# The first batch's Newton steps on PE and ACT alone, and two pieces of G inside its first expert pass

## The chip, the cores and the metric

One core of a Trainium2 chip. The time is device microseconds of one execution of the whole program; the one before is the median of three runs. TensorE is called PE, VectorE DVE, ScalarE ACT, GpSimd POOL; SP issues most loads.

## The reference

Nystrom attention on 8 batches, 8 heads, 576 tokens of 64, feeding a mixture of 8 experts in which a token keeps its predecessor's expert where its local gate says so. All is in float32.

```python
q_lm, k_lm = means of 18 tokens each            # 32 landmarks
A, Bm, C = sm(q, k_lm), sm(q_lm, k_lm), sm(q_lm, k)
Z = Bm.T / (norm1(Bm) * norminf(Bm) + 1e-6)
for _ in range(6):
    Z = 2 * Z - Z @ Bm @ Z
x = A @ Z @ C @ v                                # 512 features a token
e = argmax(x @ w_gate) if fresh(x @ w_local) else the previous token's e
out = p[e] * (relu(x @ w1[e]) @ w2[e])
```

## The kernel before

Every batch goes through an attention (a list of some 33 small steps, `attention(b)`, L740) and an expert (`expert`, L525). Attention of batch 0 is written first; then a loop over batches writes the expert of batch b in 16 iterations, and between them, by due times (`at_time`, `run`), the attention steps of the next batches, some 24 iterations ahead. Each engine executes its instructions in one order of its own. That order isn't the order of the program text: a planner simulates the program and gives each engine the next instruction that is ready in its simulation, with earlier text preferred. So batch 1's attention runs in the gaps of batch 0's, and a long instruction may stand ahead of a short one that is ready a moment later.

Four heads lie side by side on 128 partitions, twice (g = 0, 1). In `scores_c` (L190) C's and Bm's scores are made, with maxima on DVE and exponentials on ACT: two of 288 columns (ec, L213), then one of 32 (bm, L215). `norms` (L248, L250 to L272) is a chain of some 13 short DVE operations from bm to nrc. `newton_first` (L279) makes E = I - c Bt Bt' (L283, L285, L286), and `newton_step` (L288) is run six times. It keeps [E | Z] side by side, multiplies both by E on PE (L292, eight 32x32 blocks, 16 matmuls in the trace), copies the new E with ACT (L295) and adds the product to Z with DVE (L296). Then `newton_w`, `newton_wt`, `newton_gate` (L298 to L321) make the matrix W that follows A; `gates`, `fresh`, `sticky`, `chosen`, `own` (L368 to L452) choose each token's expert and the batch's main one, whose number goes into `regs` (L439).

A itself: `scores_a` (L323), `a_max` (L338: a maximum on DVE, L341, and a subtraction on POOL, L342), `a_exp`, `a_norm`, `a_back`, and `a_split` (L362), which splits A into a high and a low part, ACT L364 and DVE L365.

With the number in `regs`, SP loads the expert's w1 in two halves of 1 MB (L463) and w2 in eight pieces (L498), each of which ACT and POOL split (L500, L501). `w_w1` (L466) multiplies W into w1: G, in four pieces q. Each piece is 32 matmuls (L477) into one bank of `pg` and one of `ph`; then ACT (L490) and DVE (L491) split each bank. The expert has two passes over tokens: 320 of them (blocks 2, 3 and half a block, 4), then 256. For each of 8 f, `mm1` (L504, six matmuls at L513) makes h = relu(G' A) in a `ph` bank, which takes piece f // 2 of G; one f later, L543 (blocks 0 to 3, banks `py`) and L548, L549 (block 4, bank `pg`, held over all f) multiply h by w2.

PSUM has 8 banks: `psa` 3 (name "one"), `ph` 2, `py` 2, `pg` 1. Batch 0's attention takes all of them in turn through `one`, since no expert runs yet; later ones have the three of `psa`. For batch 0 all four pieces of G stand in the text ahead of its expert (L814 to L820).

Of the kernel before, what the change touches and what calls it, by code (L numbers as in the profile page):

```python
# [9 lines left out]
F32 = mybir.dt.float32  # L10
# [12 lines left out]
M = 32  # L23
# [34 lines left out]
def nystrom_attn_then_sticky_moe(ctx, tc, qT, kT, v, wg, w12, out):  # L58
# [80 lines left out]
    spare = [(py, "py"), (ph, "ph"), (pg, "pg"), (py, "py"), (ph, "ph")]  # L139
    one = Banks(*[(psa, "one")] * 3, *spare)  # L140
# [7 lines left out]


# [40 lines left out]
    def scores_c(st, g):  # L190
# [57 lines left out]
    def norms(st):  # L248
# [23 lines left out]
        nc.vector.tensor_scalar_mul(nrc, rc, -1.0)  # L272
# [6 lines left out]
    def newton_first(st):  # L279


        ps = one.tile([P, 2, M])
# [5 lines left out]
    def newton_step(st, k):  # L288
# [4 lines left out]
        new = st["et"] = sm.tile([P, 2, 64], F32, name="et", bufs=4)  # L293
# [4 lines left out]
    def newton_w(st):  # L298
        pw = one.tile([P, 2, D])
# [5 lines left out]
    def newton_wt(b, st):  # L305

        pwt = one.tile([P, 2, P])
# [6 lines left out]
    def newton_gate(b, st):  # L314
        pg = one.tile([P, 2, 9])
# [7 lines left out]
    def scores_a(st, hf):  # L323
# [14 lines left out]
    def a_max(st):  # L338
# [23 lines left out]
    def a_split(st):  # L362
# [65 lines left out]
    def own(b, st):  # L428
# [10 lines left out]
        nc.vector.tensor_scalar(out=regs[:, b:b + 1], in0=mx[0:1], scalar1=-1.0, scalar2=float(E), op0=ALU.mult, op1=ALU.add)  # L439
# [26 lines left out]
    def w_w1(st, q):  # L466
# [3 lines left out]
        ps = [pool.tile([P, 512], F32, name=name)[:, 0:256] for pool, name in ((pg, "pg"), (ph, "ph"))]  # L470
# [33 lines left out]
    def mm1(st, f, s0, n):  # L504
# [13 lines left out]
        nc.scalar.activation(out=h[:, 0:n], in_=hp, func=AF.Relu)  # L518
        for a, e, to in ((0, m, 384), (m, n, 320)):
            if a < e:  # L520
                nc.vector.scalar_tensor_tensor(out=h[:, to:to + e - a], in0=hp[:, a:e], scalar=0.0,  # L521
                                               in1=h[:, a:e].bitcast(F32), op0=ALU.max, op1=ALU.subtract)
        return h
# [356 lines left out]
```

## Time and profile before

| | us |
|---|---|
| median of three runs | 549.0 (548.88 to 549.81) |
| the profiled execution | 545.98 |
| its span | 544.3 |
| PE busy in the span | 489.0 (90%) |
| DVE, ACT, POOL busy | 317.2, 214.5, 194.2 |
| batch 0's expert number in its register | 54.1 |
| first matmul of the expert passes | 76.4 |

The profile is one execution. Its rows give the start and the length of an instruction, or of a run of like ones, on its engine; what stands in square brackets is how long the engine stood idle ahead of it, and what ended that. The granted clock is a share of TensorE's full 2.4 GHz; 0.5 is its lower level, 1.2 GHz.

### The profile page before, as it was taken

Reading aid. Unit: us, or ns where it says so; the run is one execution under the profiler, and the core shown is the slowest. Engines: PE = TensorE matmul, PEld = TensorE weight load, DVE = VectorE, ACT = ScalarE, POOL = GpSimd, SP = SyncE. Lnnn points to the kernel's source line nnn. Section 1 sums busy time; section 2 is a strip of 40 time slices with the busy share of each in tenths; the row PEclk is TensorE's granted clock in tenths of the full one; section 3 lists DMA queues with packets and bytes.
Section 4 is the critical chain, followed back from the end, with each engine's and each line's share of the span. In section 5 each row is a group of like instructions: output and inputs, shape, how many; then the busy total and the mean of one; then the engine's idle time right before and its main releaser. Section 6 shows DMA issues by size and latency. Waiting matters only on the chain. (4 is left out here: it accounts for less than half of the span.)

```text
span 544.3 us, 12748 instructions
## 1 busy us (share of the span) xinstructions
PE 489.0 (90%) x4983; PEld 349.7 (64%) x4983; DVE 317.2 (58%) x997; ACT 214.5 (39%) x556; POOL 194.2 (36%) x203
## 2 busy tenths in 40 slices
PE   7456479999999999999999999999978996999995
PEld 2223147866676767767676677667766884678674
DVE  7878746845775478546873587346734558732321
ACT  2433342445334543356144623364234512441451
POOL 5562740643145322624162403132141402271240
PEclk9667569999999999999999999999998999899999
DMA  8745840981187214851195114711091108171220
GB/s 301 309 132 186 305 146 1 354 268 53 40 297 287 81 51 183 307 174 50 63 393 184 37 40 173 259 59 49 5 330 56 62 1 291 50 250 59 88 79 18
DMA packets 38607, 82.62 MB, mean 152 GB/s; under 512 B 3163, under 2 KB 4443, under 8 KB 37776
## 3 DMA queue, kind: packets, MB, share of 16 engines
q1 hardware_dynamic: 30656, 66.22, 35.0%
q10 hardware_dynamic: 6400, 10.49, 5.4%
q0 software_dynamic: 1488, 5.07, 2.4%
q8 instruction: 40, 0.66, 0.5%
q14 instruction: 23, 0.19, 0.1%
HBM read 66.34 MB, written 15.47 MB: 150 GB/s over the span
## 5 line engine op out<-in xcount | busy, mean ns | idle before, releaser
L543 PE MATMUL py<-wh,h 128*128 128x512 f32 x528 | 177.3, 408 | 3.3 <-ACT h L518 3.2
L501 POOL TENSOR_TENSOR wl<-raw,wh 128x512 fp32r<-128x512 f32 x72 | 97.5, 1358 | 189.4 <-ACT wh L500 189.2
L518 ACT ACTIVATE h<-ph 128x256 fp32r<-128x256 f32 (+2 forms) x136 | 55.1, 405 | 159.4 <-PE ph L513 141.5
L521 DVE SCALAR_TENSOR_TENSOR h<-ph,h 128x256 fp32r<-128x256 f32 (+1 forms) x200 | 64.3, 347 | 80.0 <-ACT h L518 79.2
L543 PEld LDWEIGHTS py<-wh,h 128*128 128x128 f32 x528 | 90.4, 188 | 24.6 <-ACT h L518 5.6
L543 PE MATMUL py<-wl,h 128*128 128x512 f32 x264 | 87.0, 395 | 0.0
L513 PE MATMUL ph<-ath,gh 128*128 128x320 f32 (+1 forms) x256 | 81.8, 320 | 0.7 <-DVE gl L491 0.7
L513 PE MATMUL ph<-atl,gh 128*128 128x320 f32 (+1 forms) x256 | 77.8, 304 | 0.0
L513 PE MATMUL ph<-ath,gl 128*128 128x320 f32 (+1 forms) x256 | 76.7, 300 | 0.0
L500 ACT CAST wh<-raw 128x512 fp32r<-128x512 f32 x72 | 44.7, 622 | 44.7 <-PE py L543 32.5
L513 PEld LDWEIGHTS ph<-ath,gh 128*128 128x128 f32 x256 | 49.2, 192 | 17.8 <-issue 8.4
L543 PEld LDWEIGHTS py<-wl,h 128*128 128x128 f32 x264 | 49.3, 188 | 11.7 <-issue 2.1
L342 POOL TENSOR_TENSOR sa<-sa,mxa 128x1152 f32<-128x1152 f32 x8 | 17.1, 2133 | 104.4 <-DVE mxa L341 86.4
L513 PEld LDWEIGHTS ph<-atl,gh 128*128 128x128 f32 x256 | 49.4, 193 | 5.7 <-issue 2.3
L513 PEld LDWEIGHTS ph<-ath,gl 128*128 128x128 f32 x256 | 49.3, 193 | 0.3
L477 PE MATMUL ph<-raw,wt 64*32 64x256 f32 x256 | 24.7, 425 | 12.8 <-DVE gl L491 5.4
L491 DVE TENSOR_TENSOR gl<-ph,gh 128x256 fp32r<-128x256 f32 x36 | 15.2, 422 | 29.6 <-ACT gh L490 29.6
L292 PEld LDWEIGHTS one<-et 32*32 32x32 f32 x704 | 13.8, 114 | 25.5 <-issue 10.5
L292 PE MATMUL one<-et 32*32 32x64 f32 (+1 forms) x704 | 22.7, 234 | 7.9 <-DVE et L296 7.9
L174 POOL TENSOR_TENSOR t<-q_t 128x288 f32<-128x288 f32 x28 | 21.4, 789 | 15.6 <-DMA q_t<-qT 10.9
L202 PE MATMUL one<-k_t,ql 64*32 64x288 f32 (+1 forms) x240 | 25.1, 482 | 1.6 <-ACT k_t L181 0.8
L548 PE MATMUL pg<-wh,h 128*128 128x512 f32 x64 | 26.4, 412 | 0.0
(286 smaller groups left out, 736.5 us busy)
## 6 DMA issues: line engine op xcount, KB each, us to landing
raw<-w SPq DMA_DIRECT2D x18, 1024.0 KB, 6.7
raw<-w SPq DMA_DIRECT2D x72, 256.0 KB, 6.2
v_t<-v SPq DMA_DIRECT2D x8, 1024.0 KB, 6.4
out<-ys ACTq DMA_DIRECT2D x32, 256.0 KB, 2.7
q_t<-qT SPq DMA_DIRECT2D x6, 1152.0 KB, 5.1
k_t<-kT SPq DMA_DIRECT2D x6, 1152.0 KB, 7.7
ad<-sa POOLq DMA_DIRECT2D x8, 576.0 KB, 7.4
q_t<-qT SPq DMA_DIRECT2D x4, 576.0 KB, 8.4
```

The lines of the kernel that those rows point to most:

```text
L174: nc.gpsimd.tensor_add(t9[:, i], src[:, a + i, :, 0:9], src[:, a + i, :, 9:18])
L202: nc.tensor.matmul(pc[hf][32 * c:32 * c + 32, 0:n], st["ql"][r, h // 2, :], st["k"][r, h // 2, 288 * hf:288 * hf + n], start=True, stop=True)
L292: each_place(lambda g, r: nc.tensor.matmul(pn[r, g, n0:64], et[r, g, 0:32], et[r, g, n0:64], start=True, stop=True))
L342: nc.gpsimd.tensor_tensor(out=sa, in0=sa, in1=mx.unsqueeze(2).broadcast_to([P, 2 * NJ, M]), op=ALU.subtract)
L477: mm = nc.tensor.matmul(ps[g][32 * c:32 * c + 32, :], st["wt"][r, g, 32 * c:32 * c + 32], w1[r, 2 * (q % 2):2 * (q % 2) + 2, a * P:a * P + ...
L500: nc.scalar.copy(out=wh, in_=raw)
L501: nc.gpsimd.tensor_tensor(out=wl, in0=raw, in1=wh.bitcast(F32), op=ALU.subtract)
L513: nc.tensor.matmul(hp, w[:, g, c], x[:, g, s0:s0 + n], start=(i == 0), stop=(i == 5))
L518: nc.scalar.activation(out=h[:, 0:n], in_=hp, func=AF.Relu)
L521: nc.vector.scalar_tensor_tensor(out=h[:, to:to + e - a], in0=hp[:, a:e], scalar=0.0, in1=h[:, a:e].bitcast(F32), op0=ALU.max, op1=ALU.sub ...
L543: nc.tensor.matmul(yps[k], h[:, part + i * P:part + i * P + P], w, start=(f == 0 and part == 0 and w is wh), stop=(f == NC2 - 1 and part = ...
L548: nc.tensor.matmul(yps[4], x, wh, start=(f == 0), stop=False)
```

## The change

Four things are altered. (1) Batch 0's Newton chain has banks of its own, the two of `ph`; everything else of batch 0's attention has the other six in turn. In its steps PE adds Z itself, by a second matmul with the identity into the same place, and one ACT copy takes the whole [E | Z]; there is no DVE instruction in the loop. (2) In `scores_c` of all batches bm's exponential comes first. `a_max` is ordered behind the last operation of the same batch's norms, and `a_split` behind the batch's expert number; both are orders on one engine or between engines without a wait where none is needed. (3) The pieces q = 2 and 3 of batch 0's G are written inside its first pass, at iterations 1 and 3. (4) For that, in batch 0's first pass `pg` isn't held over all f: the 64 tokens of block 4 get tiles of their own for each f (`hx`, eight buffers, with an ACT relu of their own), and all sixteen matmuls of block 4 come behind the last f.

```diff
-    spare = [(py, "py"), (ph, "ph"), (pg, "pg"), (py, "py"), (ph, "ph")]
-    one = Banks(*[(psa, "one")] * 3, *spare)
+    spare = [(py, "py"), (pg, "pg"), (py, "py")]
+    one = Banks(*[(psa, "one")] * 3, (py, "py"), (pg, "pg"), (py, "py"))
+    first_chain = Banks((ph, "ph"))
+
+    def chain(b):
+
+        return one if b else first_chain
...
+    marks = {}
+
+    def not_ahead_of(inst, mark):
+
+        if mark in marks:
+            tc.add_manual_dep(inst.ins, marks[mark], mybir.DependencyInfo(
+                mybir.DependencyClass.NoSync, mybir.DependencyReason.DATA), reason="order")
...
         nc.vector.tensor_scalar_mul(nm, mx[:, 2:4], -scale)
+        nc.scalar.activation(out=st["bm"][:, g, :], in_=pc[1][:, 288:320], func=AF.Exp, bias=nm[:, 1:2],
+                             scale=scale, accum_out=st["sb"][:, g:g + 1])
         ec = at.tile([P, 2, 288], F32, name=f"ec{g}")
...
-        nc.scalar.activation(out=st["bm"][:, g, :], in_=pc[1][:, 288:320], func=AF.Exp, bias=nm[:, 1:2],
-                             scale=scale, accum_out=st["sb"][:, g:g + 1])
...
-        nc.vector.tensor_scalar_mul(nrc, rc, -1.0)
+        marks["norms", b] = nc.vector.tensor_scalar_mul(nrc, rc, -1.0).ins.name
...
-        pn = one.tile([P, 2, 64])
+        pn = chain(b).tile([P, 2, 64])
+        new = st["et"] = sm.tile([P, 2, 64], F32, name="et", bufs=4)
+        if b == 0:
+            each_place(lambda g, r: (
+                nc.tensor.matmul(pn[r, g, n0:64], et[r, g, 0:32], et[r, g, n0:64], start=True, stop=False),
+                nc.tensor.matmul(pn[r, g, 32:64], id32[r], et[r, g, 32:64], start=False, stop=True)))
+            nc.scalar.copy(out=new[:, :, n0:64], in_=pn[:, :, n0:64])
+            return
...
-        nc.vector.reduce_max(out=mx, in_=sa, axis=AX.X)
+        not_ahead_of(nc.vector.reduce_max(out=mx, in_=sa, axis=AX.X), ("norms", b))
...
-        nc.scalar.copy(out=ah, in_=st["full"])
+        not_ahead_of(nc.scalar.copy(out=ah, in_=st["full"]), f"expert of batch {b}")
...
+        marks[f"expert of batch {b}"] = nc.vector.tensor_scalar(
+            out=regs[:, b:b + 1], in0=mx[0:1], scalar1=-1.0, scalar2=float(E), op0=ALU.mult, op1=ALU.add).ins.name
...
         h = fk.tile([P, 640], F32R, name="h", bufs=3)
-        nc.scalar.activation(out=h[:, 0:n], in_=hp, func=AF.Relu)
...
+        x = fk.tile([P, P], F32R, name="hx", bufs=NC2) if apart and m < n else h[:, 2 * P:3 * P]
+        e = m if apart else n
+        nc.scalar.activation(out=h[:, 0:e], in_=hp[:, 0:e], func=AF.Relu)
+        if e < n:
+            nc.scalar.activation(out=x[:, 0:64], in_=hp[:, m:n], func=AF.Relu)
...
                     if 4 in blocks:
 
-                        x = h[:, 2 * P:3 * P]
-                        nc.tensor.matmul(yps[4], x, wh, start=(f == 0), stop=False)
-                        nc.tensor.matmul(yps[4], x, wl, start=False, stop=(f == NC2 - 1))
+
+                        for ff in range(0 if f == NC2 - 1 else NC2, NC2) if apart else (f,):
+                            if 4 not in yps:
+                                yps[4] = pg.tile([P, DM], F32, name="pg")
+                            for w in w2[ff]:
+                                nc.tensor.matmul(yps[4], hs[ff][1], w, start=(ff == 0 and w is w2[ff][0]),
+                                                 stop=(ff == NC2 - 1 and w is w2[ff][1]))
...
         sts[0]["w1", hf] = load_w1(sts[0]["e"], hf)
-        for q in range(2 * hf, 2 * hf + 2):
-            w_w1(sts[0], q)
+        if hf == 0:
+            for q in range(2):
+                w_w1(sts[0], q)
...
-        gen = expert(st, w2s[b], PASSES, lambda k, yp, b=b, st=st: store(b, st, k, yp))
+        gen = expert(st, w2s[b], PASSES, lambda k, yp, b=b, st=st: store(b, st, k, yp), b == 0)
...
             run(b * CH + i)
+            if b == 0 and i in (1, 3):
+
+                w_w1(st, 2 + i // 2)
```

## Rows read from the trace of the kernel before

**Rows 1.** Busy time by stretches: us, engines' busy (instructions), clock, DMA share, GB/s.
```profile
38.60:54.20 15.60, 10.22 (x198) 5.82 (x202) 13.61 (x64) 6.93 (x23) 4.38 (x5) 0.79 0.44 161
54.20:76.42 22.22, 10.94 (x214) 4.70 (x206) 13.96 (x28) 9.78 (x28) 13.90 (x14) 0.58 0.78 270
65.40:71.45 6.05, 3.08 (x48) 1.29 (x48) 5.11 (x9) 1.42 (x4) 2.83 (x4) 0.50 1.03 368
116.20:172.76 56.56, 56.44 (x574) 40.51 (x567) 35.53 (x114) 24.30 (x65) 21.49 (x19) 1.00 0.48 168
```

**Rows 2.** Order of time, batch 0, softmax to norms: start, length, engine, line, tiles.
```profile
14.15 0.51 ACT L213 ACTIVATE ec<-py,nm 128x288 f32<-128x288 f32 x1
...
15.10 0.31 ACT L215 ACTIVATE bm<-ph,nm 128x32 f32<-128x32 f32 x1
...
15.66 1.34 DVE L341 TENSOR_REDUCE mxa<-sa 128x36 f32<-128x1152 f32 x1
...
17.07 2.13 POOL L342 TENSOR_TENSOR sa<-sa,mxa 128x1152 f32<-128x1152 f32 x1 [0.66 <-DVE rsc L244]
...
17.78 1.50 DVE L254 TENSOR_TENSOR bm<-bm,rsb 128x64 f32<-128x64 f32 x1
...
24.19 0.22 DVE L286 TENSOR_TENSOR et<-et,id 128x64 f32<-128x64 f32 x1
```

**Rows 3.** Two lines of the kernel in all batches: length in ns, least/median/most.
```profile
L254 DVE TENSOR_TENSOR bm<-bm,rsb x8: 216/224/1500, 17.8 to 375.2; 128x64 f32<-128x64 f32 x8
...
L365 DVE TENSOR_TENSOR atl<-at,ath x8: 1357/1359/3525, 30.4 to 428.1; 128x1152 fp32r<-128x1152 f32 x8
```

**Rows 4.** Order of time, batch 0's six Newton steps.
```profile
24.55 0.65 PE L292 MATMUL py<-et 32*32 32x64 f32 x16 [2.12 <-DVE et L286]
...
25.25 0.21 ACT L295 COPY et<-py 128x64 f32<-128x64 f32 x1 [0.78 <-PE py L292]
...
25.77 0.65 PE L292 MATMUL pg<-et 32*32 32x64 f32 x16
...
28.08 0.65 PE L292 MATMUL ph<-et 32*32 32x64 f32 x16
...
30.41 1.59 DVE L365 TENSOR_TENSOR atl<-at,ath 128x1152 fp32r<-128x1152 f32 x1 [0.25 <-ACT ath L364]
...
31.92 0.21 DVE L296 TENSOR_TENSOR et<-et,ph 128x64 f32<-128x64 f32 x1
...
36.84 0.43 PE L292 MATMUL ph<-et 32*32 32x32 f32 x16
...
38.34 0.21 DVE L296 TENSOR_TENSOR et<-et,ph 128x64 f32<-128x64 f32 x1
```

**Rows 5.** Order of time, from batch 0's expert number to its expert's first matmuls.
```profile
54.00 0.14 DVE L439 TENSOR_SCALAR regs<-mxc 1x1 int32<-1x1 f32 x1
...
60.06 0.63 PE L477 MATMUL ph<-raw,wt 64*32 64x256 f32 x1 [2.92 <-DMA raw<-w]
...
68.33 0.62 ACT L500 CAST wh<-raw 128x512 fp32r<-128x512 f32 x1 [3.43 <-DMA raw<-w]
...
69.72 0.42 DVE L491 TENSOR_TENSOR gl<-pg,gh 128x256 fp32r<-128x256 f32 x1
...
75.38 0.63 PE L477 MATMUL ph<-raw,wt 64*32 64x256 f32 x1 [2.83 <-DVE gl L491]
...
76.42 0.63 PE L513 MATMUL ph<-ath,gh 128*128 128x320 f32 x1
...
77.92 0.47 PE L513 MATMUL ph<-ath,gl 128*128 128x320 f32 x1
```

**Rows 6.** Order of time: batch 3's loads; batch 1's number, and its G.
```profile
45.36 0.34 SPq L154 DMA_DIRECT2D q_t<-qT  x1
...
100.17 0.14 DVE L439 TENSOR_SCALAR regs<-mxc 1x1 int32<-1x1 f32 x1
...
115.63 0.40 PE L477 MATMUL ph<-raw,wt 64*32 64x256 f32 x1
```

More of the change, by code (lines that the diff above doesn't have):

```diff
@@ L246, in c_v, with norms @@
         nc.vector.tensor_tensor(out=st["u"], in0=pv, in1=rs.unsqueeze(2).broadcast_to([P, 2, D]), op=ALU.mult)
-    def norms(st):
+    def norms(b, st):
         rs = sm.tile([P, 2], F32, name="rsb")
@@ L277, in each_place, with newton_first @@
                 fn(g, slice(32 * c, 32 * c + 32))
-    def newton_first(st):
-        ps = one.tile([P, 2, M])
+    def newton_first(b, st):
+        ps = chain(b).tile([P, 2, M])
         each_place(lambda g, r: nc.tensor.matmul(ps[r, g, :], st["bt"][r, g, :], st["bt"][r, g, :], start=True, stop=True))
@@ L296, in newton_step, with newton_w @@
         nc.vector.tensor_add(new[:, :, 32:64], et[:, :, 32:64], pn[:, :, 32:64])
-    def newton_w(st):
-        pw = one.tile([P, 2, D])
+    def newton_w(b, st):
+        pw = chain(b).tile([P, 2, D])
         each_place(lambda g, r: nc.tensor.matmul(pw[r, g, :], st["et"][r, g, 32:64], st["u"][r, g, :], start=True, stop=True))
@@ L305, in newton_wt @@
     def newton_wt(b, st):
-        pwt = one.tile([P, 2, P])
+        pwt = chain(b).tile([P, 2, P])
         for g in range(2):
@@ L314, in newton_gate @@
     def newton_gate(b, st):
-        pg = one.tile([P, 2, 9])
+        pg = chain(b).tile([P, 2, 9])
         for g in range(2):
@@ L502, in load_w2, with mm1 @@
         return wh, wl
-    def mm1(st, f, s0, n):
+    def mm1(st, f, s0, n, apart):
         hp = ph.tile([P, 512], F32, name="ph")[:, 0:n]
@@ L517, in mm1, with expert @@
         h = fk.tile([P, 640], F32R, name="h", bufs=3)
-        nc.scalar.activation(out=h[:, 0:n], in_=hp, func=AF.Relu)
[L519 to L523, printed above, removed]
-    def expert(st, w2, passes, store):
+        x = fk.tile([P, P], F32R, name="hx", bufs=NC2) if apart and m < n else h[:, 2 * P:3 * P]
[3 more added lines that the diff above has]
+            nc.scalar.activation(out=x[:, 0:64], in_=hp[:, m:n], func=AF.Relu)
+        nc.vector.scalar_tensor_tensor(out=h[:, 384:384 + m], in0=hp[:, 0:m], scalar=0.0, in1=h[:, 0:m].bitcast(F32),
+                                       op0=ALU.max, op1=ALU.subtract)
+        if m < n:
+            nc.vector.scalar_tensor_tensor(out=x[:, 64:128], in0=hp[:, m:n], scalar=0.0, in1=x[:, 0:64].bitcast(F32),
+                                           op0=ALU.max, op1=ALU.subtract)
+        return h, x
+    def expert(st, w2, passes, store, apart=False):
         before = None
@@ L530, in expert, with after @@
             for f in range(NC2):
-                hs[f] = mm1(st, f, s0, n)
+                hs[f] = mm1(st, f, s0, n, apart)
                 if before:
                     before()
-                def after(f=f, blocks=blocks, yps=yps, h=hs[f]):
+                def after(f=f, blocks=blocks, yps=yps, hs=hs):
+                    full = [k for k in blocks if k < 4]
+                    for k in full:
+                        if k not in yps:
+                            yps[k] = py.tile([P, DM], F32, name="py")
                     wh, wl = w2[f]
-                    for k in blocks:
-                        if k not in yps:
-                            yps[k] = (py.tile([P, DM], F32, name="py") if k < 4 else pg.tile([P, DM], F32, name="pg"))
-                    full = [k for k in blocks if k < 4]
+                    h = hs[f][0]
                     for part, w in ((0, wh), (0, wl), (384, wh)):
@@ L745, in attention @@
             lm("q", 0), lm("k", 0), lambda: scores_c(st, 0), lm("q", 2), lm("k", 2), lambda: scores_c(st, 1),
[L746 to L752 removed]
+            lambda: norms(b, st), lambda: scores_a(b, st, 0), lambda: newton_first(b, st), lambda: scores_a(b, st, 1),
+            lambda: c_transpose(st, 0), lambda: newton_step(b, st, 0), lambda: c_transpose(st, 2), lambda: a_max(b, st),
+            lambda: newton_step(b, st, 1), lambda: c_transpose(st, 4), lambda: a_exp(st), lambda: newton_step(b, st, 2),
+            lambda: c_v(st), lambda: newton_step(b, st, 3), lambda: a_norm(b, st), lambda: newton_step(b, st, 4),
+            lambda: a_back(st), lambda: newton_step(b, st, 5),
+            lambda: newton_w(b, st), lambda: newton_wt(b, st), lambda: newton_gate(b, st), lambda: gates(st), lambda: fresh(st),
+            lambda: sticky(st), lambda: chosen(st), lambda: own(b, st), lambda: a_split(b, st),
         ]
```

19 lines of the change are left out of this document (5 added, 14 removed).

## The prediction

> **What bounds the kernel now.** I read the busy time by stretches first [rows 1]. From 116.20 to 172.76 us, one expert pass of a batch, PE is busy 56.44 of 56.56 us: the eight batches' expert work is one long PE-bound piece, and nothing that lies beside it counts. Ahead of it PE is busy 10.22 of 15.60 and 10.94 of 22.22 us, at a mean granted clock of 0.79 and 0.58, so near the 1.2 GHz level much of the time. This prologue, up to the first matmul of the expert at 76.42 us [rows 5], is where time can be won; a microsecond won there moves everything behind it, except for the work of batches 1 and 2 that PE does in the prologue's gaps and that would then have to be done in PE-bound time.
>
> Next I read the time-ordered rows along batch 0's chain: the softmax of the small matrix and its norms [rows 2], the Newton steps [rows 4], then the choice of the expert (its number is in the register at 54.14), the weight load, and G, made in four pieces [rows 5]. What the reader is to see: the norms wait behind a_max (1.34 us, not needed yet) and beside GpSimd; the Newton steps wait behind the split of A on DVE; and G's four pieces, of which the first expert matmul needs only the first, take from 60.06 to 76.42 us, since each waits for the bank of the one before to be read.
>
> **Part 1, norms.** With bm's exponentials first, the second one moves from 15.10 to 14.15, where the first ec of that half now starts: 0.95 earlier. a_max, which sat between the first two operations of the norms, goes behind them: 1.34. L254 took 1.50 us beside GpSimd's 2.13 us of L342 [rows 2], against a median of 0.224 [rows 3]; with a_max later L342 is later too: 1.28. Together 3.6. Against it: scores and transposes now share six banks in place of eight, so a score transpose of batch 0 may come in between, and a_max may slip in between the norms' last operation and L285; nearest row for either is a_max itself, 1.34. Bounds of the part 1.0 to 4.9 (the upper end if L285 and L286, done at 24.41, also lose the long operation that stands between them now); I take 3.0.
>
> One rule speaks against this part. L254, two SBUF inputs, took seven times its median just while GpSimd ran [rows 2, 3]. The Trainium skill, GPSIMD Engine Reference, section 1 Specifications, says that GpSimd shares its SBUF interfaces with VectorE, with contention for instructions with two SBUF inputs. By it L286 (both inputs in SBUF) would now be the one to wait beside the delayed L342, and the part would give 3.0 - (2.13 - 0.22) = 1.1. No row shows L286 in that place; it is inside my bounds.
>
> **Part 2, six Newton steps.** Before they run from 24.41 to 38.55, 14.1 us. A step without waits is 25.77 - 24.55 = 1.22 [rows 4]. The change adds 16 matmuls of 32 columns to each (the identity times Z), worth 0.43 by the last step's row, which has that shape (bounds: nothing, if they overlap, to the 0.65 of the wide ones). It removes the DVE add: the copy on ACT ends at 25.46, the next PE starts at 25.77 after DVE, and would start some 0.05 after the copy: 0.26 less. So 1.39 a step, 8.3 for six, or 1.0 more than the clean steps of before. The gain is in the waits, 14.1 - 7.3 = 6.8. The third step starts on PE at 28.08 and its add ends at 32.13, 2.8 more than a clean step: it stood behind the split of A on DVE (1.59 us from 30.41) and that split's ACT half ahead of it. The split now comes behind the expert's number, so this goes. Of the other 4.0, which stem from PE (C times V, scores of batch 1) and from queues on ACT and DVE, I let 1.2 go. 2.8 + 1.2 - 1.0 = 3.0, bounds 0.5 to 5.5. The two banks of its own cost nothing that I can see: each step frees its bank by its one copy. The moved a_max delays softmax of A by about its shift; A in full is needed only by the gates, behind the last step, newton_w and two more matmul groups, which cover it.
>
> **Part 3, from the Newton steps to the number** (38.55 to 54.14, 15.6 us) has no edit, only other neighbours: batch 1's norms and a_max stood in DVE's queue there, with DVE the busiest engine (13.61 of 15.60 us [rows 1]), and batch 1 will be a little less far. 1.0, bounds -3 to 4. The split of A now follows the number on ACT and DVE (1.36 median, 3.52 at worst [rows 3]); behind it in the queues are G's copies, which come 8 us later anyway, after the load. Cost nothing while the load takes the 5.9 us that it took; without that cover, up to 4.7.
>
> **Part 4, G.** Before, the number is there at 54.14 and PE starts the first piece at 60.06; the second ends at 65.40, where the third stretch of [rows 1] begins; the last starts only at 75.38, after a wait of 2.83 for the bank; the expert starts at 76.42. After, the expert's first matmuls follow the second piece, so 11 us earlier relative to the number. But the second piece's copies come late: ACT stood at a weight cast that waited for its DMA until 68.33, and the second piece's residual ended at 70.14 [rows 5]. Until then both ph banks are taken, so mm1 of f=1 and the third piece can't start. I therefore count PE as free-running from 16.0 us after the number (70.14 - 54.14) with 2.0 us of mm1 done, against 22.3 after it with all pieces done. 22.3 - 16.0 + 2.0 = 8.3; less the two late pieces on PE, 1.04 each at 1.2 GHz (75.38 to 76.42), half of that at 2.4 GHz, as batch 0's first pass soon has: 1.1; that leaves 7.2. Further less the work of batches 1 and 2 that PE did between 65.40 and 71.45, 3.08 busy at a granted 0.50 [rows 1], 1.5 at full clock; as the number itself comes 7 us earlier, some of batch 1's work ahead of it stays undone too, by my estimate half as much again: 2.2, which leaves 5.0. Bounds 1.5 to 10. Block 4's matmuls, moved behind the last f of the first pass, are as many as before; the extra ACT instruction for 64 columns in eight f is beside PE work.
>
> **Part 5, queues.** Batch 3's q and k, 2.3 MB, were issued on SP at 45.36 [rows 6]. With the number 7 us earlier, at about 47, the weight load would find them ahead of it on the DMA engines. At the 270 GB/s of the stretch up to 76.42 [rows 1] they need 8.5 us. Cost 0 to 6; I take 1.2, as most of it would have passed.
>
> **Part 6, batches 1 to 7.** The first exponentials are exchanged there too (0), a_max came behind the norms already (0), but the split of A waits for the number: one DVE operation of 1.36 us, 3.52 beside GpSimd [rows 3], moves from the start of the previous expert pass to its middle. Cost -0.1 to 2.2 a batch; nearest to the median, 0.2 for six batches: 1.2.
>
> **Sum.** 3.0 + 3.0 + 1.0 + 5.0 - 1.2 - 1.2 = 9.6 us. The profiled execution took 545.98 us for a span of 544.3, 3.0 below the median of the three runs, 549.0. 545.98 - 9.6 = 536.4; with the same 3.0 above it, 539.4. I say 539.5.
>
> **Rivals.** (a) Batch 1 becomes the bound. Its number is there at 100.17 and its own G starts at 115.63 [rows 6], 15.5 us later, where the load needs 5.9: 9.5 us of slack. An earlier expert pass of batch 0 eats this slack, and also puts expert matmuls in PE's queue ahead of batch 1's Newton steps. If its number slides by 4 us, only 5.5 can be kept: 543.5. For it: batch 1's steps stood in PE's order with nothing else beside them; against: the planner can place its G later in the second pass. (b) Everything comes at its upper end on the chain (parts 1 to 3 give 12, part 4 gives 8, no collision): 549.0 - 19 = 530. (c) Slower: the split in the middle of the expert passes. ACT's half of it and DVE's 3.52 stand ahead of h's production, which feeds PE at once; if PE loses the full 2.2 in each of seven batches, 15.4 go against 10.8 gained in the other parts, and it is 553.6. It decides from 1.5 us a batch. For it: the rows at 3.52 and 1.50; against: the median of the eight splits lies at their minimum, and PE has attention matmuls to fill in. (d) The change doesn't act: the order is planned from simulated times, so q2 and q3 may stay ahead, or Newton may wait elsewhere; the gain of part 4 is gone and batch 1's work and collision take parts 1 to 3: 549.
>
> **Numbers.** Forecast, 536 to 542: 0.50. (a) 0.20, (b) 0.15, (c) 0.09, (d) 0.06. About 0.2% (1.1 us) is what a measurement can tell from no change. Faster 0.85, same 0.06, slower 0.09. The range takes in (a) and half of (b): 530 to 546.5.
>
> **What would show it.** The number of batch 0 in its register near 47 us, norms done by 19, no DVE instruction between Newton copies and the next PE, six steps in 11 us; the first expert matmul 11 to 13 us after the number; the third piece between f=0 and f=1 without PE idle for over 5 us; batch 1's number before 98. Wrong would make it: a weight load that lands more than 8 us after the number, batch 1's G waiting for its weights at the end of the first expert, or the split at 3.5 us in most batches with PE idle behind h.

## The result, and the profile after

The changed kernel takes 546.16 us (median, 545.45 to 546.96) beside 548.96 for the kernel before: ratio 0.9947, 95% interval 0.9928 to 0.9966. It is faster by 0.5%, 2.8 us where 9.5 were forecast. The two profiled executions lie closer together than the medians, 545.45 and 545.98 (spans 543.6 and 544.3): the rows below can account for 0.7 of the 2.8, and the rest lies in executions without a profile. The kernel before was timed again beside each set of experiments, and its median was 548.97, 547.07, 547.28 and 546.80; the change was timed beside 548.96 alone. So each kernel below is compared by its ratio to the runs before beside it, not by its time.

Stretches of the profile after (columns: length; busy time and instructions of PE, its weight loads, DVE, ACT, POOL; granted clock, DMA share, GB/s): the Newton steps, newton_w to the number, the number to the first matmul of the expert, and the pass of batch 2. The second and third compare with the first two of [rows 1]; the pass took 58.5 us before.

```profile
23.90:44.00 20.10, 14.12 (x310) 7.73 (x310) 15.97 (x42) 6.87 (x27) 11.20 (x14) 0.50 0.43 158
44.00:62.20 18.20, 10.91 (x242) 7.66 (x238) 14.87 (x48) 5.57 (x16) 10.40 (x11) 0.59 0.49 165
...
62.20:72.58 10.38, 5.09 (x66) 1.52 (x58) 5.13 (x13) 3.82 (x12) 3.07 (x3) 0.66 0.86 302
...
174.90:232.29 57.39, 57.02 (x600) 41.12 (x599) 36.70 (x116) 25.13 (x66) 20.87 (x19) 1.00 0.48 170
```

Batch 0's chain after, in order of time: the last operations of norms and newton_first (compare [rows 2]), copies of the Newton steps (compare [rows 4]), then the number and the first matmuls of G and of the expert (compare [rows 5]).

```profile
18.74 0.69 PE L215 MATMUL one<-k_t,ql 64*32 64x288 f32 x8 [0.21 <-ACT ql L192]
...
20.17 0.17 DVE L285 TENSOR_SCALAR nrc<-rc 128x2 f32<-128x2 f32 x1
20.24 1.34 DVE L361 TENSOR_REDUCE mxa<-sa 128x36 f32<-128x1152 f32 x1
...
21.67 2.13 POOL L362 TENSOR_TENSOR sa<-sa,mxa 128x1152 f32<-128x1152 f32 x1 [1.76 <-DVE mxa L361]
22.29 1.58 DVE L299 TENSOR_TENSOR et<-et,id 128x64 f32<-128x64 f32 x1
...
29.43 0.50 ACT L228 ACTIVATE ec<-one,nm 128x288 f32<-128x288 f32 x1
...
29.91 0.27 ACT L311 COPY et<-ph 128x128 f32<-128x128 f32 x1
...
42.23 0.20 ACT L311 COPY et<-ph 128x64 f32<-128x64 f32 x1
...
62.09 0.13 DVE L459 TENSOR_SCALAR regs<-mxc 1x1 int32<-1x1 f32 x1
...
68.14 0.63 PE L498 MATMUL ph<-raw,wt 64*32 64x256 f32 x1 [3.61 <-DMA raw<-w]
...
71.55 0.63 PE L498 MATMUL ph<-raw,wt 64*32 64x256 f32 x1 [1.68 <-DVE gl L512]
...
72.58 0.63 PE L534 MATMUL ph<-ath,gh 128*128 128x320 f32 x1
```

The reader is to see four things. The number came at 62.22, 8.1 us later than before, not 7 us earlier. From the number to the expert's first matmul it took 10.4 us in place of 22.3. The first row is a score of batch 1: it ran at 18.74, where batch 1's first scores had run at 34.66 before. And from 23.90 to 44.00 PE ran at a granted 0.50, the 1.2 GHz level, for all of its 14.12 busy us; before, the steps' stretch (24.40 to 38.60) had 9.03 busy us at 0.55.

Most of what follows is read from the profiled executions, by this table. PE idle is the span less PE's busy time, both from the page. The events are: the number of batch 0; its expert's first matmul (mm1); block 4 of batch 0 read out of its bank by DVE, called the end of batch 0 (the expectations say "stored"); the same of batch 1; then how long batches 2 to 5 and batches 6 and 7 took, by the same event. What is behind batch 7's block 4 took 34.7 to 34.8 us in every kernel.

| kernel | ratio | span | PE busy | PE idle | number | first mm1 | batch 0 ends | batch 1 ends | batches 2-5 | 6-7 |
|---|---|---|---|---|---|---|---|---|---|---|
| before | | 544.3 | 489.0 | 55.3 | 54.1 | 76.4 | 115.1 | 173.4 | 236.1 | 100.0 |
| after | 0.9947 | 543.6 | 495.0 | 48.6 | 62.2 | 72.6 | 115.7 | 174.9 | 230.5 | 103.5 |
| g_only | 1.0143 | 551.4 | 492.9 | 58.5 | 53.7 | 65.0 | 108.4 | 170.2 | 243.5 | 103.1 |
| newton_only | 1.0199 | 554.3 | 500.1 | 54.2 | 65.7 | 93.0 | 125.8 | 185.3 | 234.0 | 100.4 |
| order_only | 0.9946 | 543.1 | 489.6 | 53.5 | 54.6 | 82.2 | 116.0 | 175.6 | 231.2 | 101.5 |
| amax_only | 0.9995 | 545.1 | 490.9 | 54.2 | 54.4 | 76.7 | 114.8 | 173.1 | 236.0 | 101.3 |
| split_only | 0.9998 | 545.2 | 492.9 | 52.3 | 52.7 | 75.2 | 113.9 | 170.0 | 235.3 | 105.1 |
| bm_only | 1.0174 | 556.3 | 496.1 | 60.2 | 65.7 | 93.0 | 126.4 | 186.3 | 234.8 | 100.5 |
| own_banks_dve | 0.9910 | 543.8 | 494.0 | 49.8 | 59.4 | 71.0 | 114.4 | 173.9 | 231.9 | 103.2 |
| pe_add_8banks | 0.9983 | 545.7 | 494.3 | 51.4 | 61.5 | 73.7 | 116.3 | 175.6 | 230.9 | 104.5 |
| hold_scores | 0.9933 | 541.7 | 490.8 | 50.9 | 59.9 | 71.5 | 115.0 | 174.3 | 230.9 | 101.8 |
| hold_number | 1.0044 | 548.5 | 490.4 | 58.1 | 45.7 | 56.0 | 99.4 | 181.1 | 232.0 | 100.7 |
| own_L1 | 1.0053 | 549.4 | 496.5 | 52.9 | 60.3 | 71.6 | 115.9 | 180.1 | 235.1 | 99.4 |
| undo_newton | 1.0174 | 556.3 | 499.7 | 56.6 | 54.7 | 70.8 | 114.1 | 175.3 | 237.4 | 108.8 |
| undo_g | 1.0317 | 557.7 | 500.9 | 56.8 | 61.1 | 83.7 | 119.1 | 178.7 | 239.3 | 105.0 |
| undo_bm | 1.0158 | 551.5 | 496.7 | 54.8 | 59.8 | 71.1 | 112.9 | 174.3 | 236.8 | 105.6 |
| undo_split | 1.0080 | 551.6 | 496.6 | 55.0 | 65.4 | 81.5 | 120.7 | 181.7 | 233.7 | 101.4 |
| undo_amax | 0.9879 | 537.2 | 488.8 | 48.4 | 59.9 | 70.4 | 111.8 | 170.9 | 231.1 | 100.3 |

After against before, the span's 0.7 is made of 1.5 us lost up to the end of batch 1, 5.6 won in batches 2 to 5 and 3.5 lost in batches 6 and 7. Counted the other way, PE idles 6.7 us less and is busy 6.0 us more. Of the 6.0, 4.7 lie ahead of batch 1's end (144.9 against 140.2 us, with 96 more matmuls for the addition, and at a mean granted clock of 0.844 in place of 0.852) and 1.3 in batches 6 and 7.

### The profile page after: what moved, and what is told of

It is laid out like the page before. It is cut to its first block, busy times and chain, and to the rows that moved or that the text cites. A ratio compares the mean times of both kernels' runs of the same rounds, so it can differ in the third digit from the quotient of the medians.

```text
span 543.6 us, 12936 instructions
## 1 busy us (share of the span) xinstructions
PE 495.0 (91%) x5079; PEld 354.4 (65%) x5079; DVE 318.3 (59%) x991; ACT 215.2 (40%) x565; POOL 188.2 (35%) x203
## 3 DMA queue, kind: packets, MB, share of 16 engines
q1 hardware_dynamic: 30656, 66.22, 34.7%
## 5 line engine op out<-in xcount | busy, mean ns | idle before, releaser
L570 PE MATMUL py<-wh,h 128*128 128x512 f32 x528 | 180.3, 412 | 1.8 <-ACT h L541 1.8
L522 POOL TENSOR_TENSOR wl<-raw,wh 128x512 fp32r<-128x512 f32 x72 | 92.3, 1288 | 198.6 <-ACT wh L521 196.6
L541 ACT ACTIVATE h<-ph 128x256 fp32r<-128x256 f32 (+2 forms) x136 | 54.8, 403 | 146.1 <-PE ph L534 138.2
L570 PEld LDWEIGHTS py<-wh,h 128*128 128x128 f32 x528 | 92.7, 190 | 26.4 <-ACT h L541 7.1
L544 DVE SCALAR_TENSOR_TENSOR h<-ph,h 128x256 fp32r<-128x256 f32 (+1 forms) x136 | 56.0, 412 | 80.0 <-ACT h L541 76.9
L534 PE MATMUL ph<-ath,gh 128*128 128x320 f32 (+1 forms) x256 | 80.5, 314 | 1.1 <-DVE gl L512 0.8
L362 POOL TENSOR_TENSOR sa<-sa,mxa 128x1152 f32<-128x1152 f32 x8 | 17.1, 2133 | 95.1 <-DVE mxa L361 79.7
L215 PE MATMUL one<-k_t,ql 64*32 64x288 f32 (+1 forms) x240 | 29.4, 477 | 1.0 <-ACT k_t L194 0.7
L187 POOL TENSOR_TENSOR t<-k_t 128x288 f32<-128x288 f32 x28 | 20.2, 740 | 19.9 <-DVE sq L188 16.2
L498 PE MATMUL pg<-raw,wt 64*32 64x256 f32 x256 | 26.4, 409 | 0.0
L593 ACT ACTIVATE ys<-py,pall 128x512 f32<-128x512 f32 x32 | 20.3, 686 | 14.4 <-PE py L570 14.3
L313 PE MATMUL one<-et 32*32 32x64 f32 (+1 forms) x672 | 19.7, 226 | 6.0 <-DVE et L316 3.5
```

The lines of the kernel that those rows point to most:

```text
L187: nc.gpsimd.tensor_add(t9[:, i], src[:, a + i, :, 0:9], src[:, a + i, :, 9:18])
L215: nc.tensor.matmul(pc[hf][32 * c:32 * c + 32, 0:n], st["ql"][r, h // 2, :], st["k"][r, h // 2, 288 * hf:288 * hf + n], start=True, stop=True)
L362: nc.gpsimd.tensor_tensor(out=sa, in0=sa, in1=mx.unsqueeze(2).broadcast_to([P, 2 * NJ, M]), op=ALU.subtract)
L498: mm = nc.tensor.matmul(ps[g][32 * c:32 * c + 32, :], st["wt"][r, g, 32 * c:32 * c + 32], w1[r, 2 * (q % 2):2 * (q % 2) + 2, a * P:a * P + ...
L522: nc.gpsimd.tensor_tensor(out=wl, in0=raw, in1=wh.bitcast(F32), op=ALU.subtract)
L534: nc.tensor.matmul(hp, w[:, g, c], x[:, g, s0:s0 + n], start=(i == 0), stop=(i == 5))
```

## Experiments

The diffs are against the kernel that each paragraph names.

### Edits (3) and (4) alone, the Newton parts singly, batch 1 held back

Two theories stood against each other for the late number: that the edits of batch 0's chain are slow by themselves (16 more matmuls a step), or that batch 1's work, no longer short of banks, now stands ahead of them in the queues. **g_only** is the changed kernel with edits (1) and (2) taken out:

```diff
...
-        return one if b else first_chain
+        return one
...
-        if b == 0:
+        if b < 0:
...
-        not_ahead_of(nc.scalar.copy(out=ah, in_=st["full"]), f"expert of batch {b}")
+        nc.scalar.copy(out=ah, in_=st["full"])
```

> The kernel before with edits (3) and (4) alone: the last two pieces of G inside the first pass, block 4 last. Queue theory (the two own banks of the Newton chain leave the shared banks to batch 1, whose scores then stand ahead of batch 0's steps): the chain is as before, the number at 54 us, the first expert matmul 10 to 11.5 us behind it, near 65; the time 2 to 6 us under before. Rival (PE work of batches 1 and 2 is only put off, so the earlier start is given back within the first pass whatever the chain does): first expert matmul near 65, but time within 1 us of before.

Measured: 1.0143 (1.0087 to 1.0199). The number came at 53.65, G's two pieces and the first mm1 at 65.04, 11.4 us later: part 4 does what it says, and batch 0 ends 6.7 us sooner. At the end of batch 1, 3.3 of them are left. Yet the whole is slower by 1.4%, which neither side expected: batches 2 to 5 take 243.5 us in place of 236.1.

**own_banks_dve**, against the changed kernel, leaves batch 0's chain its own banks and gives the addition back to DVE:

```diff
-        if b == 0:
+        if b < 0:
             each_place(lambda g, r: (
```

> The kernel after, but Newton's add is on DVE again, as before; the two banks of its own stay. Queue theory: batch 1's first score matmul still starts before 26 us, the six steps still take 16 us or more, and the number is at 56 to 62. Rival (the added matmuls with the identity make the steps long): the steps fall to 12 us or less and the number to about 52.

**pe_add_8banks** keeps the addition on PE and gives the banks back:

```diff
-    spare = [(py, "py"), (pg, "pg"), (py, "py")]
-    one = Banks(*[(psa, "one")] * 3, (py, "py"), (pg, "pg"), (py, "py"))
+    spare = [(py, "py"), (ph, "ph"), (pg, "pg"), (py, "py"), (ph, "ph")]
+    one = Banks(*[(psa, "one")] * 3, *spare)
...
-        return one if b else first_chain
+        return one
```

> The kernel after, but the Newton chain of batch 0 takes its banks in turn from all eight again; the add stays on PE. Queue theory: batch 1's scores move back behind the fourth step, the six steps take 9 to 12 us and the number is at 48 to 54. Rival (added matmuls): steps stay at 16 us or more, number near 60.

**hold_scores** leaves the change as it is and orders batch 1's scores behind the last Newton matmul of batch 0:

```diff
-                nc.tensor.matmul(pc[hf][32 * c:32 * c + 32, 0:n], st["ql"][r, h // 2, :],
+                mm = nc.tensor.matmul(pc[hf][32 * c:32 * c + 32, 0:n], st["ql"][r, h // 2, :],
...
+                if b == 1:
+                    not_ahead_of(mm, ("newton", 5))
```

> The kernel after, with batch 1's first scores ordered on PE behind batch 0's last Newton matmul (an order without a wait); everything else is the same. Queue theory: six steps in 9 to 12 us, the number at 48 to 54, time 2 to 8 us under the kernel after. Rival (added matmuls, or a_max and GpSimd's hold on DVE): steps stay at 16 us or more.

Measured: 0.9910 (0.9879 to 0.9940), 0.9983 (0.9960 to 1.0006) and 0.9933 (0.9914 to 0.9953). With undo_newton below, which has edits (2) to (4) and neither half of (1), the time from the end of newton_first to the start of newton_w's result on DVE is a two by two table, and so is the number:

| end of newton_first to newton_w, us | shared banks | own banks |
|---|---|---|
| add on DVE | 12.5 (undo_newton) | 18.8 (own_banks_dve) |
| add on PE | 13.8 (pe_add_8banks) | 22.5 (after) |
| number, add on DVE | 54.7 | 59.4 |
| number, add on PE | 61.5 | 62.2 |

The bare step costs what was forecast. In hold_scores, in order of time, the PE starts of steps 3 to 6:

```profile
26.17 0.46 PE L312 MATMUL ph<-et 32*32 32x64 f32 x8 [1.41 <-ACT et L315]
...
27.46 0.46 PE L312 MATMUL ph<-et 32*32 32x64 f32 x8 [0.40 <-ACT et L315]
...
28.82 0.46 PE L312 MATMUL ph<-et 32*32 32x64 f32 x8 [0.46 <-ACT et L315]
...
30.17 0.36 PE L312 MATMUL ph<-et 32*32 32x32 f32 x8 [0.45 <-ACT et L315]
```

They are 1.29, 1.36 and 1.35 us apart. What made the steps late is the pair of own banks. In all eight kernels of the table that have it and don't hold batch 1 back, batch 1's first score starts at 17.7 to 18.9 and the time of the two by two table is 18.8 to 22.5 us; in the eight with shared banks, it starts at 30.6 to 34.7 and the time is 12.5 to 16.0. That the three banks of `psa` are what was free for batch 1 is read from the code; that its scores, maxima and exponentials then stood in PE's and ACT's order is in the rows. For the steps the second theory holds.

For the number it isn't enough: with the add on PE it came at 61.50 from shared banks (48 to 54 expected), and at 59.86 in hold_scores (the same expected). What is won in the steps is lost from newton_w to the number, 24.4 and 23.6 us there against 15.0 before and 15.8 after. DVE's rows of that stretch in hold_scores hold what batch 1 had been kept from:

```profile
43.56 1.35 DVE L365 TENSOR_REDUCE mxa<-sa 128x36 f32<-128x1152 f32 x1
...
45.37 1.77 DVE L416 TENSOR_SCALAR fr<-lg 128x5 f32<-128x5 f32 x1
...
50.42 1.33 DVE L374 TENSOR_REDUCE rsa<-sa 128x36 f32<-128x1152 f32 x1
...
55.29 1.55 DVE L449 TENSOR_TENSOR ohb<-ecol,desc 128x40 bf16<-128x40 f32 x1
```

L416 and L449 are links of batch 0's chain, with medians of 0.16 and 0.20 us over the batches; L365 and L374 are batch 1's. pe_add_8banks has the same four there (1.35, 1.77, 1.33 and 1.55 us). The stretch from newton_w to the number, in pe_add_8banks and in hold_number below, where batch 1 comes behind the number:

```profile
37.15:61.50 24.35, 14.66 (x255) 8.42 (x245) 21.41 (x71) 6.04 (x23) 10.40 (x12) 0.57 0.39 139
...
34.39:45.66 11.27, 4.86 (x65) 2.74 (x69) 7.20 (x34) 2.42 (x6) 2.86 (x4) 0.50 0.04 12
```

DVE is busy 21.41 us in the one and 7.20 in the other. So batch 1's work makes the number late in either place: between the steps where it has banks early, behind them where it hasn't.

### Edit (2) alone, whole and in its three parts

The question was where the 2.8 us came from, if not from the prologue. **order_only** is the kernel before with edit (2); **amax_only**, **split_only** and **bm_only** have one part of it each:

```diff
...
+        not_ahead_of(nc.vector.reduce_max(out=mx, in_=sa, axis=AX.X), ("norms", b))
...
+        not_ahead_of(nc.scalar.copy(out=ah, in_=st["full"]), f"expert of batch {b}")
...
+        nc.scalar.activation(out=st["bm"][:, g, :], in_=pc[1][:, 288:320], func=AF.Exp, bias=nm[:, 1:2],
+                             scale=scale, accum_out=st["sb"][:, g:g + 1])
         ec = at.tile([P, 2, 288], F32, name=f"ec{g}")
```

> The kernel before with edit (2) alone: bm's exponential first, a_max behind the norms, the split of A behind the number. Theory now: of all kernels run, those with edit (2) had batch 0's number at 59 to 62 us and expert passes some 57.4 us apart, those without it at 54 us and 58.4 us or more apart; so edit (2) sets both: number at 58 to 63, passes 57 to 58 us apart, time 543 to 549. Rival (the Newton edit and its banks set the number): number at 48 to 54.

> The kernel before with a_max ordered behind the norms, alone. If a_max is what makes the number late (its GpSimd subtraction then lies beside later DVE work of the chain): norms done by 20.5, number at 58 to 62, passes 58.4 us apart as before. If it isn't: number at 51 to 54.

> The kernel before with the split of A ordered behind the expert's number, alone. If the split's place sets the steady state: passes 57 to 58 us apart, time 541 to 546, number at 50 to 54 (3 us of DVE and ACT work gone from the chain). If it doesn't: passes 58.4 apart and more.

> The kernel before with bm's exponential ahead of C's, alone. My forecast has it 0.95 us earlier at the norms and nothing else: number at 53 to 54, passes 58.4 us apart, time within 1 us of before. If it sets the late number: 58 or more.

Measured: 0.9946 (0.9927 to 0.9965) for the whole of (2), which is the ratio of the whole change; 0.9995 (0.9977 to 1.0013), 0.9998 (0.9977 to 1.0018) and 1.0174 (1.0140 to 1.0207) for its parts. No part alone brings a gain. The theory that edit (2) sets the number failed: 54.62 for the whole, where 58 to 63 was expected. And bm's exponential alone, from which no more than 1 us was expected, puts the number at 65.7; newton_w to the number takes 27.2 us there, with DVE busy 24.2. The three together win 4.9 us in batches 2 to 5, with the first mm1 5.8 us later than before.

What those passes lost before is idle time. Batches 2 to 5 as one stretch, before and after:

```profile
173.44:409.52 236.08, 229.11 (x2408) 164.01 (x2397) 139.03 (x454) 99.26 (x258) 76.42 (x65) 1.00 0.42 147
...
174.91:405.43 230.52, 229.06 (x2415) 164.94 (x2413) 139.44 (x450) 98.92 (x256) 72.57 (x64) 1.00 0.43 149
```

PE is busy 229.1 us in both, and idle for 7.0 before and 1.5 after. PE's waits from 80 us on show for what (engine, line, what for: us in total, times, longest). Of the kernel before:

```profile
PE ph L477 <- DVE ys L566: 4.7, 3, 4.1
PE py L543 <- ACT h L518: 3.2, 4, 1.1
```

Of after:

```profile
PE one L313 <- DVE et L316: 2.2, 5, 0.8
PE py L570 <- ACT h L541: 1.8, 2, 1.0
...
PE ph L498 <- DVE ys L597: 1.0, 3, 0.5
```

The 4.1 us are G of batch 6, which waited from 405 us on for the bank of block 4, at the end of batch 5's pass. In order_only the longest such wait is 1.0, in amax_only 4.0. Of the 3.2 for h, 2.2 lie in batches 2 to 5, and 0.7 there were for gl: 7.0 together.

PE also changes less often between expert matmuls and others: over the passes of batches 2 to 4, 120 times after and 121 in order_only, 154 before, and the time that expert matmuls cover in them falls from 135.0 to 131.7 us, 3.3 us over 34 changes. In the pass of batch 2, in which 599 matmuls begin in either kernel, PE is busy 57.8 us before, with 52 changes, and 57.0 after, with 40. Over all of batches 2 to 5 this saving doesn't show in the busy time: 2414 matmuls begin there after, and 2396 before. Single rows of the kernel before show the price: a like pair of matmuls in a pass, right behind attention matmuls and not.

```profile
403.44 0.73 PE L543 MATMUL py<-wh,h 128*128 128x512 f32 x2
404.01 0.63 PE L543 MATMUL py<-wl,h 128*128 128x512 f32 x2
404.47 0.62 PE L543 MATMUL py<-wh,h 128*128 128x512 f32 x2
```

So 0.07 to 0.1 us a change is an estimate from these; it was not measured by itself, and own_L1 below shows that the count doesn't rule the time.

### Batch 1 out of the way, and a grouped list

The forecast's first premise was that a microsecond won ahead of the expert moves everything behind it. **hold_number** tests it: the change, with batch 1's scores ordered behind batch 0's number.

```diff
...
+                if b == 1:
+                    not_ahead_of(mm, "expert of batch 0")
```

> The kernel after, with batch 1's first scores ordered behind batch 0's expert number (an order without a wait). Queue theory of the prologue (batch 1's and batch 2's instructions ahead of batch 0's on DVE, PE and ACT make the chain long): steps in 9 to 13 us, newton_w to the number in 11 to 14 us where hold_scores took 23.5, number at 46 to 50, first expert matmul at 57 to 61. If PE's work is only put off, block 4 of batch 0 is still stored no earlier than 112 us (115.7 after) and the time lies within 3 us of the kernel after.

Measured: 1.0044 (1.0022 to 1.0066). Batch 0's chain does what was forecast of it: the number at 45.66 (forecast near 47), the first mm1 at 56.01, batch 0's end 15.7 us sooner than before. All of it is given back in the next pass, by stretches:

```profile
56.00:99.40 43.40, 40.10 (x434) 28.53 (x426) 25.47 (x71) 17.22 (x58) 17.40 (x17) 0.96 0.39 140
99.40:122.20 22.80, 14.18 (x264) 8.27 (x263) 18.88 (x71) 7.20 (x20) 8.41 (x7) 0.68 0.54 194
```

From 99.40 on PE has hardly an expert matmul left: it has batch 1's chain, whose number comes at 114.28 (100.31 before), some attention of batch 2, and then waits for the weights:

```profile
122.21 0.63 PE L500 MATMUL ph<-raw,wt 64*32 64x256 f32 x1 [2.10 <-DMA raw<-w]
```

PE is busy for 14.18 of 22.80 us there, and batch 1 ends at 181.1, 7.7 us later than before. So the premise doesn't hold as it stands: work of batch 1 that is put off behind batch 0's number costs all that batch 0 wins, and more. The order that holds batch 1 back is itself the cause here; in g_only, where nothing is held, half of batch 0's 6.7 us was still there at the end of batch 1.

**own_L1** was meant to cut the changes on PE further: own_banks_dve with a batch's steps of one kind side by side in the list.

```diff
-            lambda: norms(b, st), lambda: scores_a(b, st, 0), lambda: newton_first(b, st), lambda: scores_a(b, st, 1),
-            lambda: c_transpose(st, 0), lambda: newton_step(b, st, 0), lambda: c_transpose(st, 2), lambda: a_max(b, st),
-            lambda: newton_step(b, st, 1), lambda: c_transpose(st, 4), lambda: a_exp(st), lambda: newton_step(b, st, 2),
+            lambda: scores_a(b, st, 0), lambda: scores_a(b, st, 1), lambda: norms(b, st), lambda: newton_first(b, st),
+            lambda: c_transpose(st, 0), lambda: c_transpose(st, 2), lambda: c_transpose(st, 4), lambda: newton_step(b, st, 0),
+            lambda: a_max(b, st), lambda: newton_step(b, st, 1), lambda: a_exp(st), lambda: newton_step(b, st, 2),
```

> The kernel after with Newton's add on DVE again, and for all batches the attention's steps written in groups: both halves of A's scores ahead of the norms, the three transposes of C together. Its plan has 283 changes on PE, 20 fewer than own_banks_dve, whose ratio to before was 0.991. Switch theory: passes 56.5 to 57.2 us apart, time 540 to 544. Rival (switches don't matter): passes 57.4 or more, time as own_banks_dve or slower.

Measured: 1.0053 (1.0023 to 1.0084), with 112 changes in those three passes, the fewest of all, where 540 to 544 us were expected of them. Batch 1's pass alone took 64.2 us, with PE busy 58.4, against 59.5 and 58.8 in own_banks_dve. Fewer changes are no gain where waits come in their place.

### One edit alone, or one taken out

**newton_only** is the kernel before with edit (1); **undo_newton** (edit (1)), **undo_g** (edits (3) and (4)), **undo_bm**, **undo_split** and **undo_amax** are the changed kernel with one edit taken out. Their lines are those of the diffs above, and for G:

```diff
-        if hf == 0:
-            for q in range(2):
-                w_w1(sts[0], q)
+        for q in range(2 * hf, 2 * hf + 2):
+            w_w1(sts[0], q)
...
-        gen = expert(st, w2s[b], PASSES, lambda k, yp, b=b, st=st: store(b, st, k, yp), b == 0)
+        gen = expert(st, w2s[b], PASSES, lambda k, yp, b=b, st=st: store(b, st, k, yp))
...
-            if b == 0 and i in (1, 3):
-
-                w_w1(st, 2 + i // 2)
```

> The kernel before with edit (1) alone, Newton's banks and add. Its plan has 343 changes on PE, as many as before. Switch theory: passes 58.4 us apart; the time within 3 us of before, whatever the number does. Rival (the Newton edit carries the gain): 545 or less with passes as before.

> The kernel after without the order that puts the split of A behind the number. In its plan PE changes 357 times between expert matmuls and other matmuls, 303 times in the kernel after, 343 before. Switch theory (each change costs PE about 0.1 us, and that is what sets the distance of the expert passes): passes 58.5 to 59.5 us apart, time 549 to 554. Rival (the split's own place on DVE and ACT, or the start of the expert, sets the time): passes near 57.4, time 545 to 548.

> The kernel after without edit (1): Newton's add on DVE, banks in turn from all eight. If the edits add up (edit (1) alone cost 11 us): 9 to 12 us faster than the kernel after, 535 to 538. If only the order that comes out counts: its plan has 329 changes on PE against 303, 2 to 3 us slower than the kernel after by 0.1 us a change, 546 to 550; its prologue like order_only's, number at 54 to 56, as edit (2) with eight banks has it.

> The kernel after without edits (3) and (4): all of batch 0's G ahead of its expert, block 4 as before. If the edits add up (they alone cost 8 us): 538 to 541. If only the order counts: 325 changes on PE, 2 to 3 us slower than the kernel after, 546 to 550, the first expert matmul at 82 to 93 as in the two kernels with all of G ahead and a late number.

> The kernel after with bm's exponential last again. If the edits add up (it alone cost 9 us): 536 to 540. If only the order counts: 327 changes on PE, 2 to 3 us slower than the kernel after; norms done 0.5 to 1.0 us later.

> The kernel after with a_max free to stand ahead of the norms. Alone that order made no difference (0.9995). Its plan has 303 changes on PE, as the kernel after: within 1.5 us of the kernel after, passes 57.4 us apart, norms of batch 0 done 1 to 2 us later and its last DVE operation before the steps back at 0.22 us in place of 1.58.

Measured: 1.0199 (1.0172 to 1.0227) for (1) alone; 1.0080 (1.0055 to 1.0105) without the split's order, 1.0174 (1.0126 to 1.0222) without (1), 1.0317 (1.0292 to 1.0343) without (3) and (4), 1.0158 (1.0129 to 1.0188) without bm first, and 0.9879 (0.9840 to 0.9917), 539.19 us, without a_max's order. Every edit but (2) is a loss alone, every one but a_max's order is needed beside the others: the edits don't add. Both sides of the expectations missed undo_newton, undo_g and undo_bm: none is faster than the change by what its edit costs alone, and none just 2 to 3 us slower, but 2.1 to 3.7% by the ratios. newton_only, expected within 3 us of before, is 2.0% slower, and undo_amax, expected within 1.5 us of the change, is 0.7% faster by the ratios. undo_split alone came in at the time expected from its count of changes, but with passes 57.1 to 59.2 us apart and not 58.5 or more. So the count of changes isn't what sets the time. In the five that lose PE is busy 7.6 to 11.9 us longer than before (6.0 in the change itself), and in undo_newton, undo_g and undo_bm the passes come in pairs, a long and a short one. Of undo_newton, by stretches from one block 4 to the next:

```profile
175.34:232.27 56.93, 56.39 (x521) 39.43 (x521) 34.71 (x114) 23.71 (x64) 19.52 (x18) 1.00 0.47 164
232.27:293.34 61.07, 59.81 (x685) 43.40 (x681) 36.52 (x117) 26.01 (x70) 23.32 (x21) 1.00 0.49 167
```

One pass holds 685 matmuls and the next 521, where after has 600 in each; the pair takes 118.0 us against 114.6. An edit in batch 0 has moved attention work of all later batches, as the planner orders the whole program anew. Why it falls into pairs there, the runs don't tell.

undo_amax beats both kernels. It has the instructions of after, 5079 matmuls on PE in either, and PE idles as long, 48.4 and 48.6 us; but PE is busy 488.8 us and not 495.0, at a mean granted clock of 0.948 and not 0.936. The difference lies where the clock is low: up to the end of batch 1, 140.8 and 144.9 us busy at 0.870 and 0.844; in batches 6 and 7, 91.9 and 94.0 at 0.966 and 0.951; in batches 2 to 5, 229.1 in both, at 1.00. Over all executions undo_amax ran at 0.939 to 0.948, the change at 0.931 to 0.936. Undo_amax, from the end of newton_first to newton_w, and from batch 6's block 4 to batch 7's:

```profile
23.59:44.12 20.53, 12.15 (x302) 6.88 (x302) 18.35 (x43) 6.17 (x26) 12.03 (x14) 0.68 0.55 192
...
457.30:502.40 45.10, 44.72 (x298) 35.78 (x298) 17.16 (x49) 16.99 (x38) 16.52 (x15) 0.96 0.35 114
```

After, the latter stretch:

```profile
459.95:508.96 49.01, 46.83 (x298) 37.32 (x298) 17.28 (x50) 16.93 (x38) 16.49 (x15) 0.92 0.32 106
```

The first is 0.68 against 0.50 in after's first row above, for nearly as many matmuls; the second has 298 in both, 2.1 us busy time more, and 1.8 us more idle. That a_max's order itself holds the clock down isn't shown: its place changes the plan of everything behind it.

## Why the prediction was right in sign and wrong in size

The sum can be followed by the rows. Parts 1 to 3 put the number 8.1 us later, where 7.0 earlier was forecast: this is the step that failed. From the number to the end of batch 0 it took 53.5 us in place of 61.0, 7.5 won where parts 4 and 5 had 3.8; from there to the end of batch 7, 393.3 in place of 394.4, 1.1 won where part 6 had a loss of 1.2. Together some 0.6, the 0.7 of the span but for rounding and the tail. That the sign came out right is luck: of the forecast's gains the largest block turned into a loss, and what made up for it in batches 2 to 5 was not in the sum.

**Part 1, norms (3.0 forecast, 0.5 measured, under its bound of 1.0).** nrc was there 1.8 us sooner, where 3.6 were counted for the norms; bm's second exponential began at 14.72, 0.4 earlier and not 0.95. But a_max, which the order allows directly behind nrc, took its 1.34 us there, and L299 then took 1.58 beside L362, where L254 had taken 1.50 beside L342 before [rows 2, 3] and L299's median over the batches is 0.20. The stall didn't go; it changed its victim. In undo_amax it falls on L282 of the norms, a tensor_scalar, with 1.58 again (from 20.48 to 22.06; POOL's operation ends at 22.04), and newton_first ends at 23.59, earlier than after. The failed terms are the 1.28 that L254's wait was to give back and the 1.34 of a_max, which came back behind nrc, as the prediction had named possible. The Trainium skill, GPSIMD Engine Reference, section 1 Specifications, weighed in the prediction, states contention on shared SBUF interfaces between GpSimd and VectorE instructions with two SBUF inputs. The trace agrees: L299, the L286 of before, ends at 23.87 and L362 at 23.80. L282 has one SBUF input, so this part of the rule doesn't cover it; why it waited, no run shows.

**Part 2, Newton (3.0 forecast, a loss of 7.8 measured).** This is the largest miss. The step was sized well: 1.39 forecast, 1.29 to 1.36 in hold_scores. What failed is the sentence that two banks of its own cost nothing. Eight shared banks had kept batch 1 back; with own banks its first scores went from 34.66 to 18.74, and the copy of step 2 at 29.91 came behind its exponentials. PE, ACT and DVE each have one order, and the chain met in it the work that the old banks had kept out. But giving the banks back would not have saved the forecast: the number came at 61.50 in pe_add_8banks, as the chain met batch 1 on DVE behind the steps.

**Part 3, to the number (1.0 forecast, a loss of 0.8 measured)** lay inside its bounds; the reason did not hold, since batch 1 was further ahead, not less far.

**Part 4, G (5.0 forecast).** From the number to the first mm1 10.4 us, 11 to 13 forecast; from 74 to 90 us PE was busy 13.46 of 16.00 with the two late pieces in between. The mechanism is right, in after and in g_only. The first mm1 came 3.8 us sooner in spite of the late number. From the number to the end of batch 0, 7.5 us were won, inside the bounds; that isn't the edit's alone, as a late number leaves PE more of batch 1's work ahead of it, and g_only, with the number as before, won 6.2. The late number took it all: batch 0 ended at 115.68 (115.11 before), with PE busy 86.1 us up to there, 82.0 before, at a mean clock of 0.76 and 0.78.

**Part 5, queues.** Batch 3's loads went out at 39.80 and the number came so late that they had passed: 5.9 us from the number to G's first matmul, as before. Cost 0, inside the bounds.

**Part 6, batches 1 to 7 (a loss of 1.2 forecast).** The sign was wrong. The split took 1.34 to 1.35 us in all eight batches, never 3.52 [rows 3], and batches 2 to 5 took 4.9 us less with edit (2) alone and 5.6 less in the change, of which batch 1 and batches 6 and 7 gave back 4.4. It was priced as one DVE operation that moves, while the planner moved the attention work of every batch with it.

**The sum.** It added terms ahead of the expert as if each moved all behind it, and set one estimate against that, 2.2 us for batches 1 and 2. hold_number shows how far off that can be: 20.4 us won at the first mm1 end as 4.2 us lost in the span. The prologue is shared by two batches; PE-bound time begins only when batch 1 is through as well. hold_number is rival (a) come true, with batch 1's number 14.0 us late. In the change itself (a) did not act: batch 1's number came at 99.14, 1.2 us earlier than before. Half of rival (d) came true, Newton waiting elsewhere. Rival (c) did not.

**What stays open.** Why single edits fall into plans that are slower by 1 to 3%; why the three parts of edit (2) win in batches 2 to 5 together and not singly; and what makes up the 2.1 us between the medians' gain and the traces'. The profiled execution before, 545.98, lies below all five that were timed beside the change (547.62 to 549.81), so the traces may understate the gain.

## What to carry to other kernels

Before a chain is given buffers of its own, ask whom the shortage of buffers was holding back: that work will come into the same queues ahead of the chain. Price a gain in a shared prologue by when the last of its users is through, not the first, and at the clock that its rows show. Where a planner orders the program, an edit has no price of its own: run the parts alone and left out, and keep the best plan, here the change without one of its orders.

## What was not expected of the hardware

Several small DVE operations took as long as a long GpSimd one beside them still ran: 1.58 us in place of 0.20 (L299, two SBUF inputs) and 1.58 us for a tensor_scalar with one (L282), 1.77 us for L416 in hold_scores, which began at 45.37 beside GpSimd's operation of 44.99 to 47.11. A pair of 128x512 matmuls took 0.73 us right behind attention matmuls of 32 output columns and 0.62 or 0.63 in the rows behind, at full granted clock (1.00 from 397.0 to 405.4). And the same 5079 matmuls took PE 488.8 us in one order and 495.0 in another, at mean granted clocks of 0.948 and 0.936.
